# Combining the range flag on VectorE, reading it earlier, and splitting the last PSUM copy between VectorE and ScalarE

## The chip, the cores and the metric

The kernel runs on one core of a Trainium2 chip. TensorE (PE in the profile) multiplies matrices into the accumulator memory PSUM; VectorE (DVE), ScalarE (ACT) and GpSimd (POOL) work element by element on PSUM and on the on-chip memory SBUF; SyncE (SP) issues DMA transfers and computes nothing. Each engine runs its own instruction queue in order, and semaphores tie the queues together. The metric is the device time of one execution in microseconds (us).

## The reference

The reference is attention inside chunks of 64 positions, followed by a two-layer feed-forward block with an exact GELU. There are 8 batches, 8 heads, 576 positions (nine chunks) and 64 channels a head.

```python
scores = scale * np.matmul(q_c, k_c.transpose(0, 1, 2, 4, 3))
scores = scores - np.max(scores, axis=-1, keepdims=True)
attn = np.exp(scores)
attn = attn / (np.sum(attn, axis=-1, keepdims=True) + 1e-09)
out = np.matmul(attn, v_c)
...
x = np.ascontiguousarray(attn_out.transpose(0, 2, 1, 3)).reshape(B * S, H * D)
h = x @ w_in
g = 0.5 * h * (1.0 + erf(h * inv_sqrt2))
return (g @ w_out).astype(np.float32)
```

x is 4608 x 512, w_in 512 x 2048, w_out 2048 x 512, all float32.

## The kernel before

The 4608 rows are worked through in nine tiles of 512 rows: tiles 0 to 7 hold the first eight chunks of one batch each, tile 8 the ninth chunk of all eight batches. For a tile the kernel makes the scores, takes exp without subtracting the maximum, divides by the sums, and sends the result through the two layers in bf16. From tile 1 on, both layers are computed by seven block products instead of eight (a Strassen scheme), so VectorE makes sums and differences of blocks, and results are put together from products. The order on each engine is written out by hand: tables of step names (`LAST` is that of tile 8) and hooks that hang work on the slots of the second layer.

**The last tile's second layer** (`mm2_seven`) has seven steps of two slots each, 14 slots numbered from 0; a slot is eight matmuls of 128 x 256 into one PSUM tile `y_ps`, accumulated. For the last tile the bank called "a" is two PSUM tiles, one for each 128 rows. A step's result is copied by ScalarE into a `kept` buffer (L721), or added by VectorE to such a buffer (L726), which `store_block` then stores (L874). The last step ends in `last_piece`, once for each 128 rows: VectorE copies the 128 x 256 result out of PSUM (L978), and two transfers of 64 KB store it, one issued by SyncE, one by ScalarE (L981).

**The range flag.** Leaving out the maximum is exact enough only while the sums are in range. All reciprocals of sums stay in SBUF in three places. At slot 6 of the last tile's second layer, `range_test` takes their minima and maxima on VectorE (L885), compares these with 2^-40 and 2^40 (L886, L887), and reduces the comparisons to one value a partition, 1 for good (L888). After the last step `range_count` adds the 128 values by a matmul with ones (L894), and VectorE casts the sum to an integer (L895). All five engines then load it into a register (`values_load`, L1337) and branch (L1338): below 128, the whole computation is done once more in a general way (`general`), which these inputs do not need; else they go to the end of the program, where SyncE waits for every semaphore in turn and all engines meet.

Of the kernel before, what the change touches and what calls it, by code (L numbers as in the profile page):

```python
# [11 lines left out]
def kernel(  # L12
# [9 lines left out]
    nc = tc.nc  # L22
    P = 128
    f32 = mybir.dt.float32
    bf16 = mybir.dt.bfloat16
# [7 lines left out]
    G = H // 2  # L33
# [27 lines left out]
    QD = P // G  # L61
# [17 lines left out]
    NB = MT // 32  # L79
    late = rest[:].bitcast(f32)[:, 256 - 14 * NB:256]  # L80
    homes = [None, ident_f[:], late]
# [26 lines left out]
    work = ctx.enter_context(tc.tile_pool(name="work", bufs=3))  # L108
# [5 lines left out]
    ps_at = ctx.enter_context(tc.tile_pool(name="ps_at", bufs=3, space=bass.MemoryType.PSUM))  # L114
# [329 lines left out]
    DV, AC, PO = nc.vector.tensor_copy, nc.scalar.copy, nc.gpsimd.tensor_copy  # L444
# [84 lines left out]
    HD = d_model // 2  # L529
    HM = MT // P // 2  # L530
# [343 lines left out]
            by.dma_start(rows.rearrange("m p d -> p m d"), y_sb[i * CH:(i + 1) * CH])  # L874

    LOW, HIGH = 2.0 ** -40, 2.0 ** 40
    verdict = []

    def range_test():

        assert used == [h.shape[-1] for h in homes]
        n = len(homes)
        for a, op in enumerate((mybir.AluOpType.min, mybir.AluOpType.max)):
            for i, home in enumerate(homes):
                nc.vector.tensor_reduce(ends[:, a, i:i + 1], home, axis=mybir.AxisListType.X, op=op)  # L885
        nc.vector.tensor_scalar(ok[:, 0:n], ends[:, 0], LOW, None, op0=mybir.AluOpType.is_gt)  # L886
        nc.vector.tensor_scalar(ok[:, n:2 * n], ends[:, 1], HIGH, None, op0=mybir.AluOpType.is_lt)  # L887
        nc.vector.tensor_reduce(good, ok, axis=mybir.AxisListType.X, op=mybir.AluOpType.min)  # L888
        verdict.append(good)

    def range_count():

        count = ps_at.tile([1, 1], f32, tag="at", name="count")
        nc.tensor.matmul(count[:], ones_1, verdict[0], start=True, stop=True)  # L894
        nc.vector.tensor_copy(total, count[:])  # L895

    def general():

# [76 lines left out]

    def last_piece(t, m, y_ps):
        y_sb = ypool.tile([P, HD], f32, tag="y", name="y_sb")
        DV(y_sb[:], y_ps)  # L978
        for i in range(P // CH):
            m0 = ((HM + m) * (P // CH) + i) * S + MT  # L980
            (nc.sync if i == 0 else nc.scalar).dma_start(out[m0:m0 + CH, 0:HD], y_sb[i * CH:(i + 1) * CH])  # L981
# [47 lines left out]
    def phase(t, extra2, by_rows=False, first=0, extra1={}, seven=False):  # L1029
        nms = MT // P  # L1030
        order = [(ms, qt) for ms in range(nms) for qt in range(NQ)]
        if by_rows:
            order = [(None, f) for f in range(FF - FC)] + [(ms, NQ - 1) for ms in range(nms)]
        if t not in DENSE:
            mm1_seven(t, extra1)
        else:
            for f in range(first, FF):
                for u in extra1.get(f, ()):
                    u()
                mm1_slot(t, f)  # L1040
        if seven:
            mm2_seven(t, extra2)
            return
        for s, (ms, qt) in enumerate(order):
            for u in extra2.get(s, ()):
                u()
            if ms is None:
                mm2_rows(t, qt)
            else:
                mm2_slot(t, ms, qt)  # L1050
        for u in extra2.get("end", ()):
            u()
# [33 lines left out]
    act_scratch = consts.tile([P, 1], f32, name="act_scratch")  # L1086
    small = consts.tile([P, 28], f32, name="small")
    ends = small[:, 0:6].rearrange("p (a i) -> p a i", a=2)
    ok, good, ones_1 = (small[:, 6:11].bitcast(bf16)[:, a:b] for a, b in ((0, 6), (6, 7), (7, 8)))
    total = small[0:1, 11:12].bitcast(mybir.dt.int32)  # L1090
    nc.gpsimd.memset(ones_1, 1.0)
    homes[0] = consts.tile([P, 3 * NB + 16 + 2 * NB], f32, name="early")[:]

    def act_table(func):
# [2 lines left out]
    with tc.manual_schedule():  # L1097
# [158 lines left out]
        for t in range(1, NT):  # L1256
            n = t + 1
            if n < NT:
                tiles[n]["x"] = xpool.tile([P, G, MT], bf16, tag="x", name="x")
            if t == 2:  # L1260
                sums_home()
            if t in STEPS:
                play(t, STEPS[t])
                continue
            if t == 1:
                mm1_slices(1, {0: mm, 1: at, 2: at, 3: mm, 8: mm},
                           (((0, 1, 2), (0,)), last_av, ((0, 1, 2), (1,)), ((3,), (0, 1)), ((8,), (0, 1)),
                            ((0, 1, 2, 3, 8), (2,)), ((0, 3, 8, 1, 2), (3,))))
                x_sums(1)
                for g in range(G):  # L1270
                    cast_qk(2, "k", g, DV)
                flip(2, "q")
                load_v_rows(2, (0,))
                flip(2, "k")
                for ms, y_sb in held:
                    store(0, ms, y_sb)
                held.clear()
                load_v_rows(2, (1,))
                cast_v_rows(2, PO)
                bring_qk(3)  # L1280
            if t > T0 and n + 1 < NT:
                flip_qk(n + 1)
            def next_loads():
                if t + 3 == NT - 1:
                    bring_qk(t + 3)
                elif t + 3 < NT:
                    bring_qk(t + 3)
                if n + 1 < NT:
                    load_v_rows(n + 1)
                    cast_v_rows(n + 1, PO)  # L1290
            if t == T0:
                flip(n + 1, "q")
            elif t > T0:
                next_loads()
            e1, e2 = {}, {}
            exp, gelu = lambda: act_table(Act.Exp), lambda: act_table(Act.Gelu)
            xs = [lambda m=m: quad_x(n, m // 2, m % 2) for m in range(G)]
            g = [[lambda i=i, a=a: g_sum(t, i, a) for i in (1, 2, 4)] for a in range(2)]
            parts = [[lambda m=m: quad_part(t + 2, m // 2, m % 2) for m in ms] for ms in ((1, 0), (3, 2))]
            e1 = {"s3": [lambda: g_sum(t, 3)], "g0": g[0]} if t not in DENSE else {9: [lambda: g_sum(t, 3)], 13: g[0]}  # L1300
            e2 = {0: g[1][:2], 2: g[1][2:]}
            if t <= T0:
                ov = [lambda m=m: quad_over(n, m) for m in range(G)]
                rx = [[lambda m=m: att_rc(n, m), lambda m=m: quad_x_plain(n, m)] for m in range(G)]
                e2 = {0: [exp, lambda: quad_scores(n, ALONE)] + g[1][:2], 2: g[1][2:],
                      4: [lambda: [quad_sums(n), quad_turned(n)]], 5: [ov[0]], 6: [ov[1]],
                      7: [ov[2]] + rx[0], 8: [ov[3]] + rx[1], 9: rx[2], 10: rx[3]}
                e2[{1: 7, 2: 5, T0: 6}[t]].insert(1, lambda: quad_av(n, ALONE))
                if t > 1:
                    e1["x"] = [lambda: x_sums(t)]  # L1310
                if t == T0:
                    e1["g0"] = g[0][:1] + [lambda: w_in_sums(3, (0, 1))] + g[0][1:] + [lambda: w_in_sums(3, (2, 3))]
                if t == 1:
                    e1["w"] = [lambda: weight_sum(2), lambda: weight_sum(3)]
                    e1["w0"] = [lambda: w_in_sums(0, (0, 1))]
                    e1["w1"] = [lambda: w_in_sums(0, (2, 3))]
                    e2[2].append(lambda: weight_sum(4))
                    e2[4].append(lambda: load_qk(4, "q"))
                    e2[7].append(lambda: pool_cast_qk(4, "q"))
                    e2[12] = [lambda: flip_qk(3), lambda: load_qk(4, "k"), lambda: pool_cast_qk(4, "k"),  # L1320
                              lambda: load_v_rows(3), lambda: cast_v_rows(3, PO)]
                else:
                    e1["k"] = [lambda: flip_qk(n + 1) if t < T0 else flip(n + 1, "k"), next_loads]
                if t < T0:
                    e2[11] = [gelu]
                else:
                    e2[2] += [lambda: g_sum(t, 3)]
                    e2[10] += [lambda: quad_scores(n + 1, BETWEEN), gelu]
                    e2[12] = [lambda: x_sums(n)] + parts[0]
                    e2[13] = parts[1]  # L1330
            if t in WHOLE:
                e1, e2 = whole_hooks(t)
            if t == NT - 1:
                e2.setdefault(6, []).append(range_test)
            phase(t, e2, first=5 if t == 1 else 0, extra1=e1, seven=True)
        range_count()
        in_range = nc.values_load(total)  # L1337
        with tc.If(in_range < P, preferred_fallthrough_block=False):  # L1338
            general()
# [1 line left out]
_INS = ['q', 'k', 'v', 'moe_w_in', 'moe_w_out']  # L1341
# [26 lines left out]
```

## Time and profile before

| | us |
|---|---|
| Median of three runs (lowest, highest) | 266.9 (266.48, 267.42) |
| The profiled execution's own time | 267.09 |
| Its span, first to last instruction | 265.5 |
| TensorE busy in the span | 256.1 |
| VectorE busy | 223.1 |
| ScalarE busy | 190.5 |
| GpSimd busy | 103.2 |

Busy times are of instructions that compute. Loading a register, branching, waiting for a semaphore and issuing a DMA are a sequencer's work and are not counted there; the profile shows them under names such as SPq or ACTq, by line. In a timeline row stand the start, the duration, engine, line, operation, result and source. In a row of groups, the count is followed by total busy time and the mean in ns, then by the idle time before.

### The profile page before, as it was taken

What the parts mean: (1) busy time and instruction counts of PE and PEld (TensorE: products, weight loads), DVE (VectorE), ACT (ScalarE), POOL (GpSimd) and SP (SyncE); (2) the same over time, 40 slices, a digit from 0 to 9 for tenths busy, and PEclk for the clock granted to TensorE, in tenths of its full rate; (3) what the DMA queues carried; (4) which work ended last, traced back from release to release, by engine and by line L of the source; (5) the groups of instructions that cost most, each with busy time, mean ns of one, the idle gap of its engine ahead of it and who ended that gap; (6) DMA issues with size and microseconds to landing.
All of it is one profiled execution on the core that took longest, in us unless ns stands there. A gap on an engine that the chain in (4) does not pass through costs nothing.

```text
span 265.5 us, 7854 instructions
## 1 busy us (share of the span) xinstructions
PE 256.1 (96%) x3122; PEld 210.6 (79%) x3122; DVE 223.1 (84%) x394; ACT 190.5 (72%) x386; POOL 103.2 (39%) x225
## 2 busy tenths in 40 slices
PE   6789999999999999999999999999999999999993
PEld 2478875556888888887888888888888888888882
DVE  6874986898897599678999999999999999948772
ACT  3856758987767987898888588947894789227720
POOL 7767778702364291481372095009411300000000
PEclk9999999999999999999999999999999999999998
DMA  6999998999979979999999988998973410130014
GB/s 201 268 311 396 395 401 236 283 193 289 243 195 284 220 175 244 275 239 249 276 245 232 267 186 237 217 175 195 264 160 80 134 42 2 41 119 3 2 40 125
DMA packets 123416, 54.02 MB, mean 203 GB/s; under 512 B 97776, under 2 KB 120304, under 8 KB 123376
## 3 DMA queue, kind: packets, MB, share of 16 engines
q1 hardware_dynamic: 123072, 53.23, 77.4%
q8 instruction: 25, 0.41, 0.7%
q10 hardware_dynamic: 304, 0.26, 0.3%
q14 instruction: 15, 0.12, 0.1%
HBM read 36.70 MB, written 9.44 MB: 174 GB/s over the span
## 4 chain that ended last, share of the span: by engine, by line
PE 76%; DMA 10%; ACT 7%; SPq 4%; issue 1%; DVE 0%; POOL 0%
PE hs_ps L601 31%; PE y_ps L761 22%; PE y_ps L791 13%; DMA arrival<-in_moe_w_out_dram 8%; ACT h L609 3%; SPq L181 2%; PE h_ps L491 2%; DMA arrival<-in_moe_w_in_dram 2%; PE av_ps L349 2%; PE h_ps L481 2%; ACT pT L272 2%; SPq L142 1%; PE y_ps L1025 1%; PE y_ps L989 1%; PE s_ps L264 1%; ACT L1095 1%
## 5 line engine op out<-in xcount | busy, mean ns | idle before, releaser
L609 ACT ACTIVATE h<-hs_ps 128x512 bf16<-128x512 f32 x87 | 49.6, 609 | 6.5 <-PE hs_ps L601 5.7
L238 POOL CAST v_nat<-arrival 128x256 bf16<-128x256 f32 x56 | 24.9, 473 | 33.5 <-DMA arrival<-in_v_dram 23.1
L601 PEld LDWEIGHTS <-w_in_sb 128*128 128x128 bf16 x348 | 33.9, 98 | 4.7 <-issue 0.2
L194 POOL CAST q_nat<-arrival 128x256 bf16<-128x256 f32 x40 | 16.8, 467 | 50.2 <-DMA arrival<-in_k_dram 25.3
L601 PE MATMUL hs_ps<-x,w_in_sb 128*128 128x256 bf16 x232 | 31.8, 272 | 0.0
L761 PEld LDWEIGHTS <-h 128*128 128x128 bf16 x240 | 23.2, 98 | 2.8
L1095 ACT ACT_TABLE_LOAD x16 | 20.5, 1283 | 1.3 <-PEq L1352 1.0
L190 POOL CAST k_nat<-arrival 128x256 bf16<-128x256 f32 (+1 forms) x44 | 19.1, 476 | 5.3 <-DMA arrival<-in_k_dram 5.3
L721 ACT COPY kept<-y_ps 128x512 f32<-128x512 f32 (+1 forms) x17 | 9.0, 536 | 16.0 <-PE y_ps L761 15.9
L761 PE MATMUL y_ps<-w_out_sb,h 128*128 128x256 bf16 x160 | 18.6, 273 | 0.0
L761 PE MATMUL y_ps<-v_bd,k_bd 128*128 128x256 bf16 x160 | 18.5, 273 | 0.1
L761 PEld LDWEIGHTS <-k_bd 128*128 128x128 bf16 x160 | 15.6, 98 | 2.1 <-issue 0.2
L618 ACT COPY hs_ps<-hs_ps 128x512 f32<-128x512 f32 x29 | 16.2, 583 | 0.6 <-PE hs_ps L601 0.5
L601 PE MATMUL hs_ps<-k_bd,w_in_sb 128*128 128x256 bf16 x116 | 16.6, 272 | 0.0
L493 ACT ACTIVATE h<-h_ps 128x512 bf16<-128x512 f32 x21 | 12.5, 604 | 5.5 <-PE h_ps L465 4.1
L272 ACT ACTIVATE pT<-s_ps 128x512 bf16<-128x512 f32 x28 | 14.4, 599 | 1.8 <-PE s_ps L264 1.8
L791 PEld LDWEIGHTS <-h 128*128 128x128 bf16 x144 | 13.8, 98 | 1.7
L465 PE MATMUL h_ps<-x,w_in_sb 128*128 128x256 bf16 x128 | 14.5, 273 | 0.1
L601 PE MATMUL hs_ps<-k_bd,w_in_more 128*128 128x256 bf16 x96 | 14.2, 273 | 0.0
L601 PEld LDWEIGHTS <-w_in_more 128*128 128x128 bf16 x128 | 12.5, 98 | 2.0 <-issue 0.3
L726 DVE TENSOR_TENSOR kept<-y_ps,kept 128x512 f32<-128x512 f32 (+1 forms) x16 | 10.4, 651 | 4.3 <-PE y_ps L761 2.3
L465 PEld LDWEIGHTS <-w_in_sb 128*128 128x128 bf16 x128 | 12.3, 98 | 2.1 <-DVE w_in_sb L1070 0.7
(175 smaller groups left out, 638.9 us busy)
## 6 DMA issues: line engine op xcount, KB each, us to landing
arrival<-in_v_dram SPq DMA_DIRECT2D x58, 128.0 KB, 3.2
arrival<-in_k_dram SPq DMA_DIRECT2D x28, 256.0 KB, 5.6
arrival<-in_q_dram SPq DMA_DIRECT2D x7, 1024.0 KB, 6.9
out_dram<-kept SPq DMA_DIRECT2D x24, 256.0 KB, 3.2
arrival<-in_moe_w_out_dram SPq DMA_DIRECT2D x4, 1024.0 KB, 12.1
arrival<-in_moe_w_in_dram SPq DMA_DIRECT2D x6, 512.0 KB, 8.5
out_dram<-y_sb SPq DMA_DIRECT2D x8, 256.0 KB, 2.5
arrival<-in_v_dram SPq DMA_DIRECT2D x28, 64.0 KB, 2.7
```

The lines of the kernel that those rows point to most:

```text
L190: copy(st[nm][:, q0:q0 + n, g], st[nm + "f"][:, 2 * q0:2 * (q0 + n), g].rearrange("p (q r) d -> p q r d", r=2))
L194: copy(st[nm][:, g, j:j + 2].rearrange("p j r d -> p r j d"), st[nm + "f"][:, 2 * g:2 * g + 2, j:j + 2])
L238: copy(st["v"][:, r::2, n], st["vf"][:, r::2, n])
L272: nc.scalar.activation(pT[:].rearrange("p u (c j) -> p u c j", j=J), tiles[t]["s_ps"][m // 2][m % 2][:].rearrange("p u (j c) -> p u c j", ...
L465: nc.tensor.matmul(to[:, cols], left, right[:, cols], start=(start and a == 0), stop=stop, skip_group_check=True)
L493: nc.scalar.activation(tiles[t]["h"][:, f, :], h_ps[:], Act.Gelu)
L601: nc.tensor.matmul(hs[:, f], left[:, ks, f * P:(f + 1) * P], right[:, ks], start=(fresh and f == 0 and ks == 0), stop=(ks == 1), skip_grou ...
L609: nc.scalar.activation(h[:, n:n + HM, HD * c:HD * (c + 1)], src, Act.Gelu)
L618: "s11": lambda: AC(place_of("b")[:], bank["a"][:]),
L761: nc.tensor.matmul(to, left(f, m), right[:, f], start=(fresh and (split or m == 0) and f == 0), stop=(f == HF - 1), skip_group_check=True)
L791: nc.tensor.matmul(bank[name][:, m], left(f, m), right[:, f], start=(fresh and m == 0 and f == 0), stop=(f == HF - 1), skip_group_check=True)
L1095: nc.scalar.activation(act_scratch[:], rest[:, 0:1], func)
```

## The change

`range_test` goes further on VectorE: it transposes the 128 values of the flag within blocks of 32 partitions (L889 of the changed kernel), takes the minimum of each row (L890), combines the four blocks' minima one at a time (L892), and writes an integer `bad`, 1 if the flag is below 0.5 (L893). The matmul with ones, its cast and the ones themselves are gone. The register is loaded at three places in the program: by SyncE and GpSimd at the end of `range_test`, by ScalarE at slot 10, by TensorE and VectorE after the last step. The branch takes the general way if the register is not zero. In `last_piece` the last 128 rows are copied in two halves of 128 columns, the first by VectorE, the second by ScalarE.

```diff
     def range_test():
...
-        nc.vector.tensor_reduce(good, ok, axis=mybir.AxisListType.X, op=mybir.AluOpType.min)
-        verdict.append(good)
-
-    def range_count():
-
-        count = ps_at.tile([1, 1], f32, tag="at", name="count")
-        nc.tensor.matmul(count[:], ones_1, verdict[0], start=True, stop=True)
-        nc.vector.tensor_copy(total, count[:])
+        nc.vector.tensor_reduce(good, ok, axis=mybir.AxisListType.X, op=MIN)
+        turned = work.tile([P, NB, 32], f32, tag="rc", name="turned", bufs=4)[:, 0]
+        nc.vector.transpose(turned, good.to_broadcast([P, 32]))
+        nc.vector.tensor_reduce(good, turned, axis=mybir.AxisListType.X, op=MIN)
+        for s in range(1, G):
+            nc.vector.tensor_tensor(good[0:1], good[0:1], good[QD * s:QD * s + 1], op=MIN)
+        nc.vector.tensor_scalar(bad, good[0:1], 0.5, None, op0=mybir.AluOpType.is_lt)
+        read_flag((mybir.EngineType.SP, mybir.EngineType.Pool))
+
+    flag = nc.alloc_registers("flag")
+
+    def read_flag(engines):
+        for reg in flag:
+            if reg.engine in engines:
+                nc.reg_load(reg, bad)
...
     def last_piece(t, m, y_ps):
         y_sb = ypool.tile([P, HD], f32, tag="y", name="y_sb")
-        DV(y_sb[:], y_ps)
+        n = HD // 2 if m == HM - 1 else HD
+        DV(y_sb[:, 0:n], y_ps[:, 0:n])
+        if n < HD:
+            AC(y_sb[:, n:HD], y_ps[:, n:HD])
...
-    nc.gpsimd.memset(ones_1, 1.0)
...
             if t == NT - 1:
                 e2.setdefault(6, []).append(range_test)
+                e2.setdefault(10, []).append(lambda: read_flag((mybir.EngineType.Activation,)))
             phase(t, e2, first=5 if t == 1 else 0, extra1=e1, seven=True)
-        range_count()
-        in_range = nc.values_load(total)
-        with tc.If(in_range < P, preferred_fallthrough_block=False):
+        read_flag((mybir.EngineType.PE, mybir.EngineType.DVE))
+        with tc.If(flag, preferred_fallthrough_block=False):
             general()
```

SyncE's queue at the end of the program, before. `kept` are sums of the last tile that are stored, `y_sb` its last rows, `small` the buffer that holds the flag; what a row waits for stands in brackets, by engine or by DMA queue.

```order
L874 DMA out_dram<-kept 64x2x256 [waits DMAHW0_49]
L874 DMA out_dram<-kept 64x2x256 [waits DMAHW1_49,DVE_49]
L874 DMA out_dram<-kept 64x2x256 [waits DMAHW2_49]
L874 DMA out_dram<-kept 64x2x256 [waits DMAHW4_49,DVE_49]
L981 DMA out_dram<-y_sb 64x256 [waits DMAHW6_49,DVE_49]
L981 DMA out_dram<-y_sb 64x256 [waits DMAHW0_49,DVE_49]
L1337 TENSOR_LOAD small [waits DVE_49]
L1338 COMPARE_AND_BRANCH
```

And after:

```order
L874 DMA out_dram<-kept 64x2x256 [waits DMAHW0_49]
L901 TENSOR_LOAD small [waits DVE_49]
L874 DMA out_dram<-kept 64x2x256 [waits DMAHW1_49,DVE_49]
L874 DMA out_dram<-kept 64x2x256 [waits DMAHW2_49]
L874 DMA out_dram<-kept 64x2x256 [waits DMAHW4_49,DVE_49]
L990 DMA out_dram<-y_sb 64x256 [waits DMAHW6_49,DVE_49]
L990 DMA out_dram<-y_sb 64x256 [waits DMAHW0_49,Activation_49]
L1346 COMPARE_AND_BRANCH
```

The load moved from behind the last store to ahead of the stores of the second `kept` buffer, five stores earlier, and the last store waits for ScalarE (Activation) where it waited for VectorE.

ScalarE's queue at the same place, before:

```order
L874 DMA out_dram<-kept 64x2x256 [waits DVE_49,Activation_49]
L981 DMA out_dram<-y_sb 64x256 [waits DVE_49]
L981 DMA out_dram<-y_sb 64x256 [waits DMAHW7_49,DVE_49]
L1337 TENSOR_LOAD small [waits DVE_49]
L1338 COMPARE_AND_BRANCH
```

And after:

```order
L901 TENSOR_LOAD small [waits DVE_49]
L874 DMA out_dram<-kept 64x2x256 [waits DVE_49,Activation_49]
L990 DMA out_dram<-y_sb 64x256 [waits DVE_49]
L987 COPY y_sb<-y_ps 128x128 [waits DMAHW7_49,DMAHW0_49,DVE_49]
L990 DMA out_dram<-y_sb 64x256 [waits Activation_49]
L1346 COMPARE_AND_BRANCH
```

The load now stands ahead of ScalarE's three stores, and a copy of 128 columns, which waits for VectorE, between the last two.

VectorE's queue from the last reduction of the range test to the next add, after (before, the same reduction was followed by that add at once):

```order
L887 TENSOR_REDUCE small<-small 128x1 [waits DVE_49]
L889 STREAM_TRANSPOSE turned<-small 128x32 [waits DVE_49]
L890 TENSOR_REDUCE small<-turned 128x1 [waits DVE_49]
L892 TENSOR_TENSOR small<-small 1x1 [waits DVE_49] x3
L893 TENSOR_SCALAR small<-small 1x1 [waits DVE_49]
L726 TENSOR_TENSOR kept<-y_ps,kept 128x512 [waits DMAHW5_49,PE_49,Activation_49]
```

Six instructions came in between, each of which waits for VectorE's own semaphore.

More of the change, by code (lines that the diff above doesn't have):

```diff
@@ L876 @@
     LOW, HIGH = 2.0 ** -40, 2.0 ** 40
-    verdict = []
     def range_test():
         assert used == [h.shape[-1] for h in homes]
-        n = len(homes)
+        MIN, n = mybir.AluOpType.min, len(homes)
         for a, op in enumerate((mybir.AluOpType.min, mybir.AluOpType.max)):
@@ L1088 @@
     ends = small[:, 0:6].rearrange("p (a i) -> p a i", a=2)
-    ok, good, ones_1 = (small[:, 6:11].bitcast(bf16)[:, a:b] for a, b in ((0, 6), (6, 7), (7, 8)))
-    total = small[0:1, 11:12].bitcast(mybir.dt.int32)
-    nc.gpsimd.memset(ones_1, 1.0)
+    ok, good = small[:, 6:12], small[:, 12:13]
+    bad = small[0:1, 13:14].bitcast(mybir.dt.int32)
     homes[0] = consts.tile([P, 3 * NB + 16 + 2 * NB], f32, name="early")[:]
```

## The prediction

> **What bounds the kernel now.** I read four views in this order: the page's busy shares and its chain, then the timeline of the last microseconds engine by engine, then the rows of the lines that only the sequencers run (flag load, branch, final waits), then the DMA landings. Changed work lies only at the end, so the first view has to say whether anything before it matters.
>
> ```profile
> span 265.5 us, 7854 instructions
> PE 256.1 (96%) x3122; PEld 210.6 (79%) x3122; DVE 223.1 (84%) x394; ACT 190.5 (72%) x386; POOL 103.2 (39%) x225
> 248.99 12.24 PE y_ps L761 x112
> 261.26 0.42 DVE y_sb L978
> 261.68 0.05 DVE small L895
> ```
>
> TensorE is busy 96% of the span, and the chain is TensorE to 261.2 us. So a change at the end can touch two things: whether TensorE is held up in its last steps, and what follows 261.2. After that the span has another 4.3 us (265.5 less 261.2), in which hardly any engine is busy. The chain view stops at 261.7 because sequencer work isn't in it, so I asked for it by line.
>
> ```profile
> 261.26 0.42 DVE L978 COPY y_sb<-y_ps 128x256 f32<-128x256 f32 x1 [0.45 <-PE y_ps L761]
> 261.60 0.13 DVE L895 CAST small<-count 1x1 int32<-1x1 f32 x1
> 261.71 0.49 SPq L981 DMA_DIRECT2D out_dram<-y_sb  x1
> 261.71 0.55 ACTq L981 DMA_DIRECT2D out_dram<-y_sb  x1
> L1337 POOLq TENSOR_LOAD <-small x1: 587/587/587, 261.8 to 261.8; - x1
> L1337 SPq TENSOR_LOAD <-small x1: 952/952/952, 262.2 to 262.2; - x1
> L1338 SPq COMPARE_BRANCH  x2: 38/50/61, 263.3 to 263.4; - x2
> L1363 SPq EVENT_SEMAPHORE  x12: 28/28/28, 263.9 to 264.6; - x12
> L1363 SPq DRAIN  x1: 13/13/13, 264.7 to 264.7; - x1
> ...
> out_dram<-y_sb SPq DMA_DIRECT2D x1, 64.0 KB, 1.9
> out_dram<-y_sb ACTq DMA_DIRECT2D x1, 64.0 KB, 2.2
> ```
>
> The reader is to see SyncE's own sequence. It issues the last store at 261.71, loads the flag from 262.2 to 263.2, branches at 263.3 and 263.4, reaches the end block at 263.9, and walks twelve waits to 264.6, after which the closing barrier takes the rest. The last two stores, issued at 261.71, land 1.9 and 2.2 us later, at 263.6 and 263.9. So when the walk reaches most of its waits the stores have landed: the sequencer's flag read and branch set the end, not the transfers. The count itself is not late: VectorE has it at 261.73, while SyncE is issuing until 262.2.
>
> **The change part by part.** First, the flag read leaves SyncE's end: in the order shown with the change it stands ahead of five stores, and the last store now waits for ScalarE. Call T the issue of that store. Before, the walk ends at T + 2.9 (264.6 less 261.71). After, SyncE is free for the branch at T + 0.5; from its first compare to the walk it took 0.6 (263.3 to 263.9), so the walk begins at T + 1.1 and meets transfers still under way. What is late next is the landing: T + 1.9 for SyncE's store. The twelve waits are 0.064 us apart (0.7 over 11 gaps). In the built program the fifth of them holds the semaphore of SyncE's last store and the twelfth that of ScalarE's, so seven gaps (0.45) follow the landing: T + 2.35, with ScalarE's at T + 2.2 inside it. That is 0.55 less. Bounds: were the store's wait first in the walk, T + 2.6 (0.3 less); were only the landing of 2.2 to count, 0.7 less.
>
> Second, T itself moves, since the last copy is split. In the order ScalarE's half (L987) waits for VectorE and for no matmul: it stands behind VectorE's half, and so the two halves run one after the other.
>
> ```profile
> L978 DVE COPY y_sb<-y_ps 128x256 f32<-128x256 f32 x2 | 0.8, 424 | 0.9 <-PE y_ps L761 0.9
> L613 DVE COPY kept_p<-hs_ps 128x512 f32<-128x512 f32 x2 | 1.4, 684 | 2.0 <-PE hs_ps L601 2.0
> L721 ACT COPY kept<-y_ps 128x256 f32<-128x256 f32 x4 | 1.4, 377 | 0.8 <-PE y_ps L761 0.8
> L721 ACT COPY kept<-y_ps 128x512 f32<-128x512 f32 x13 | 7.6, 584 | 15.2 <-PE y_ps L761 15.1
> L981 ACTq DMA_DIRECT2D out_dram<-y_sb x2: 553/600/648, 260.8 to 261.7; - x2
> ```
>
> VectorE pays (684 - 424)/256 = 1.02 ns a column, so 128 columns take 0.424 - 0.130 = 0.29 us; ScalarE pays 0.81 ns, so 0.377 - 0.104 = 0.27. With 0.03 from an end to the next start (the copy ends at 261.68, the store is issued at 261.71), T = 261.26 + 0.29 + 0.03 + 0.27 + 0.03 = 261.88, 0.17 later. Bounds: side by side, T = 261.58, 0.13 earlier; each half as dear as its 256-column row, 262.12, 0.41 later. I take 0.17, by the slopes of the same operations. Even without the wait ScalarE would not start at 261.26, since its previous store holds its queue from 260.84 for 0.65 us, to 261.49. The Trainium skill (PSUM — Partial Sum Buffer, section on PSUM bank collisions) says that reads by VectorE and ScalarE from one bank and quadrant collide and have to be kept apart, disjoint columns too. The wait in the order agrees with that; by it the sum takes +0.17, and without it -0.13 with ScalarE idle.
>
> Third, VectorE combines the flag by six small instructions, each waiting for the one before, which the order shows between the last reduction (L888 before) and the add at L726.
>
> ```profile
> 256.33 0.17 DVE L887 TENSOR_SCALAR small<-small 128x3 bf16<-128x3 f32 x1
> 256.54 0.16 DVE L888 TENSOR_REDUCE small<-small 128x1 bf16<-128x6 bf16 x1
> 257.82 1.24 DVE L726 TENSOR_TENSOR kept<-y_ps,kept 128x512 f32<-128x512 f32 x2 [1.12 <-PE y_ps L761]
> L410 DVE STREAM_TRANSPOSE rc<-rb 128x512 f32<-128x512 f32 x15 | 10.6, 705 | 1.4 <-ACT rb L336 1.2 <-ACT rb L403 0.2
> L287 DVE STREAM_TRANSPOSE pt<-pT 128x256 f32<-128x256 f32 x16 | 6.9, 434 | 0.0
> L895 DVE CAST small<-count 1x1 int32<-1x1 f32 x1 | 0.1, 134 | 0.0
> L726 DVE TENSOR_TENSOR kept<-y_ps,kept 128x512 f32<-128x512 f32 x1 | 0.7, 693 | 1.1 <-PE y_ps L761 1.1
> L726 DVE TENSOR_TENSOR kept<-y_ps,kept 128x256 f32<-128x256 f32 x2 | 0.8, 424 | 0.6 <-PE y_ps L761 0.4
> L761 PE MATMUL y_ps<-v_bd,h x16: 272/272/273, 259.3 to 260.9; 128*128 128x256 bf16 x16
> ```
>
> The transpose: 0.434 - 224 x 1.06 ns = 0.20. The reduction of 32 columns: 0.18, a little over the 0.16 of L888. The four single-element steps have no row of their kind; between 0.13 (the cast) and 0.17 (L887), 0.16 each. A dependent step began 0.04 after the one before ended. So 0.20 + 0.18 + 4 x 0.16 + 6 x 0.04 = 1.26 us, from 256.70 to 257.96, in an idle stretch that ended at 257.82: the add starts 0.14 late. Its cover: the first add takes 0.69 us, to 258.51, and the pair ends at 259.06, so the second (0.42) began at 258.64 and the first has 0.13 us to spare; TensorE's last step begins at 259.3 in the bank that the second frees, which is another 0.24. Cost 0. If the cover went, each further microsecond would reach TensorE whole.
>
> Fourth, what the moved loads hold up. SyncE's load starts at about 257.96 and takes between 0.59 (POOL's row) and 0.95 (its own, right behind a store); I take 0.6, as its queue is idle then. Behind it stand the stores of the first add, which went out at 258.54 and 259.19, and of the second pair at 259.96:
>
> ```profile
> 256.01 0.37 ACT L721 COPY kept<-y_ps 128x256 f32<-128x256 f32 x1 [0.50 <-PE y_ps L761]
> 258.54 1.25 SPq L874 DMA_DIRECT2D out_dram<-kept  x2
> 259.96 0.59 SPq L874 DMA_DIRECT2D out_dram<-kept  x1
> 260.02 0.74 ACTq L874 DMA_DIRECT2D out_dram<-kept  x1
> ```
>
> The add itself is done at 258.66 now, so they go 0.14 later, or 0.4 later by the dear load. The next y_sb store, due at 260.83, is met either way (258.91 + 3 x 0.6 + gaps = 260.8). ScalarE's load sits between its last copy (done at 256.4) and 260.02: hidden. POOL has no work left; TensorE's and VectorE's loads follow their last work, as before. Gone with no gain are the count matmul and its cast, since SyncE was issuing until 262.2, and a one-column memset on POOL at the start, which is 0% of the chain.
>
> Sum: -0.55 + 0.17 + 0 = -0.38 us on the profiled execution's 267.09 (its span 265.5 and 1.6 around it). That one is 0.19 above the median of 266.9, so I forecast 266.9 - 0.38 = 266.5 us. 0.3% of this kernel is 0.8 us, about what a measurement can tell from no change; the forecast is within it.
>
> **The rivals.** (a) Side by side: the halves do not queue on each other. For it: both read 128 columns of their own. Against: the wait, and ScalarE's issue to 261.49. It gives -0.55 - 0.13, 266.2.
>
> (b) The gain is eaten by the transfers, and the change so doesn't shorten the end. For it:
>
> ```profile
> 259.60:261.60 2.00, 1.71 (x16) 1.28 (x14) 1.10 (x4) 0.00 (x0) 0.00 (x0) 1.00 0.71 169
> 261.60:263.50 1.90, 0.00 (x0) 0.00 (x0) 0.13 (x2) 0.00 (x0) 0.00 (x0) 1.00 0.80 235
> ...
> DMA to landing us min/median/max: 1.9/2.2/2.4
> ```
>
> The last stores run with the DMA engines 71% and 80% busy; stores that go out up to 0.4 us later share the same end. Against: the four y_sb stores land in 1.9 to 2.4 us, the last pair no later than the pair ahead of it. If the landing slips by 0.38 the time is 266.9.
>
> (c) More than I count: only the landing of 2.2 limits (-0.7), and T holds or comes earlier (0 to -0.13): 266.1 or a little less, the faster side.
>
> (d) Slower: the small steps on VectorE are dearer than their rows. Place: the add at 257.82. It reaches TensorE when the chain passes 1.12 + 0.13 + 0.24 = 1.49 us, 0.25 a step, and makes the kernel slower than before at 1.87 (0.31 a step), by 0.8 us at 2.67 (0.44 a step, a 256-column transpose's price); then 267.7. Against: the 0.13 to 0.17 of the nearest rows.
>
> (e) The branch is slower among the stores. SyncE's jump took 0.5 (263.4 to 263.9) when the transfers were ending; now it falls at about 262.5, among them.
>
> ```profile
> q14 instruction: 3, 0.02, 2.5%
> q8 instruction: 1, 0.02, 2.1%
> ```
>
> In the last 3 us the one packet of the instruction queue q8 took 2.1% of 16 engines, 1.0 us. The walk's fifth wait would be reached at T + 1.35 and the landing is at T + 1.9, so a jump may take 0.55 more unseen: one such packet is free, two in a row (2.0) start the walk at T + 2.6 and end it at T + 3.3, 0.95 above the forecast: 267.5. Beside it the Trainium skill (Runtime: NRT & Kernel Launch, section on instruction fetch mechanics): a taken branch outside the fetched window stalls for a DMA of the target page.
>
> **How the numbers follow.** Forecast 0.50, (a) 0.10, (b) 0.15, (c) 0.12, (d) 0.07, (e) 0.06. Faster by over 0.3%: (c), and as much again from (a) and the forecast, whose bounds reach 266.1: 0.22. Slower: most of (d) and (e) with the dear ends of the split, 0.10. Same: 0.68. The range takes in (a), (b) and most of (c): with the 0.9 us that three runs of one kernel already spread (266.48 to 267.42), 265.9 to 267.2; outside remain parts of (c), (d) and (e).
>
> **What would show it.** In the changed kernel's profile: SyncE's flag load near 258.0 with about 0.6 us; ScalarE's L987 starting after VectorE's L985 ends, near 261.6, and the last stores issued near 261.9; SyncE's end waits starting near 263.0 and finishing near 264.2; the six small VectorE rows ending by 258.0 and TensorE's last y_ps step still starting at 259.3. I am wrong if the last step starts later, if the walk still begins after 263.8, or if the last landing takes clearly over 2.2 us.

## The result

The changed kernel takes 268.15 us in the median of 16 runs (267.15 to 269.12), the kernel before 266.81 (265.98 to 267.81). The ratio is 1.0042, with a 95% interval of 1.0026 to 1.0058: slower by 0.7 to 1.5 us, where 0.4 us less was forecast. Nearly everything in the forecast's sum came out; one term that it held fixed, the time a store takes to land, did not.

The profiled execution of the changed kernel (268.19 us, its span 266.6) shows this in its last microseconds. First the timeline, columns as before:

```profile
258.00 0.14 DVE L893 TENSOR_SCALAR small<-small 1x1 int32<-1x1 f32 x1
258.11 1.21 DVE L726 TENSOR_TENSOR kept<-y_ps,kept 128x512 f32<-128x512 f32 x2
...
261.51 0.29 DVE L985 COPY y_sb<-y_ps 128x128 f32<-128x128 f32 x1 [0.45 <-PE y_ps L761]
261.88 0.27 ACT L987 COPY y_sb<-y_ps 128x128 f32<-128x128 f32 x1 [5.24 <-DVE y_sb L985]
262.17 0.50 ACTq L990 DMA_DIRECT2D out_dram<-y_sb  x1
```

Then the rows of the flag loads, of the branches, and of SyncE's walk through the twelve end waits (here the whole walk, behind it the same line asked for up to 264.5 us and up to 265.3 us only, and last the row that has TensorE's first instruction behind its branch, a DRAIN at 262.0):

```profile
L901 SPq TENSOR_LOAD <-small x1: 469/469/469, 258.2 to 258.2; - x1
L901 PEldq TENSOR_LOAD <-small x1: 513/513/513, 260.3 to 260.3; - x1
L1346 PEldq COMPARE_BRANCH  x2: 90/200/310, 260.9 to 261.7; - x2
L1346 SPq COMPARE_BRANCH  x2: 38/50/61, 262.7 to 262.8; - x2
L1371 SPq EVENT_SEMAPHORE  x12: 28/28/28, 263.3 to 265.7; - x12
...
L1371 SPq EVENT_SEMAPHORE  x4: 28/28/28, 263.3 to 263.5; - x4
...
L1371 SPq EVENT_SEMAPHORE  x5: 28/28/28, 263.3 to 265.3; - x5
...
L1371 PEldq DRAIN  x2: 8/160/311, 262.0 to 266.2; - x2
```

SyncE reaches its walk 1.1 us after the last store's issue, as forecast (263.3 less 262.17). But it gets through only four waits; the fifth, for its own last store, opens at 265.3, and the twelfth comes at 265.7, 3.5 us after the issue. The kernel before took 2.9. The landings say why:

```profile
DMA to landing us min/median/max: 2.3/3.1/3.2
...
out_dram<-y_sb SPq DMA_DIRECT2D x1, 64.0 KB, 3.1
out_dram<-y_sb ACTq DMA_DIRECT2D x1, 64.0 KB, 3.2
```

Before, these two stores landed 1.9 and 2.2 us after issue. What kept them stands in the DMA queues. Packets, MB and share of the 16 DMA engines, first from 263.0 to 264.25 us, then from 264.1 to 265.0:

```profile
q1 hardware_dynamic: 77, 0.06, 19.8%
q10 hardware_dynamic: 85, 0.07, 19.7%
q8 instruction: 1, 0.02, 6.1%
q14 instruction: 2, 0.02, 3.9%
...
q1 hardware_dynamic: 5, 0.00, 3.6%
q10 hardware_dynamic: 5, 0.00, 1.8%
```

One instruction packet on queue q8 took 6.1% of 16 engines in 1.25 us: 1.22 us, nearly a whole engine for the whole window. It starts at 263.01 and so ends at 264.23. From 264.04 to 264.21 no store packet starts; then come five packets of each store queue (q1 is SyncE's, q10 ScalarE's). A store of 64 KB is 64 rows of 1 KB, four to each of 16 engines, and a flag write each: five packets are one engine's share. The trace doesn't name a packet's engine, but the count and the moment fit one reading: fifteen engines had delivered their part in time, and the one with the instruction packet delivered last. (The two packets of q14 start at 264.04 and 264.07, when the other shares are through; an experiment below has the same hold without them.) In the kernel before, the packet came later, and so did TensorE's branch, which is in the last row:

```profile
q14 instruction: 3, 0.02, 7.0%
q8 instruction: 1, 0.02, 5.8%
...
L1338 PEldq COMPARE_BRANCH  x2: 91/198/304, 262.5 to 262.8; - x2
```

The queue rows are of the kernel before from 263.8 to 264.9: 1.0 us of q8 again (5.8% of 16 times 1.1), with no store packet left in the window. Little was to spare: the last store packet starts before 263.6, q8's at 263.84.

The packet follows a branch, and TensorE's is the branch that fits. In the kernel before TensorE branched from 262.5 to 262.8, since its flag came from VectorE's cast at 261.7. Now it loads the flag at 260.3, while its matmuls still run, and branches from 260.9 to 261.7 (rows above). The sequence on one engine moved ahead by 1.1 us and q8's packet by 0.8, onto the last stores. The profile shows no wait of TensorE for this packet: its first instruction behind the branch runs at 262.0, a microsecond before the packet starts.

### The profile page after: what moved, and what is told of

It is laid out like the page before. It is cut to its first block, busy times and chain, and to the rows that moved or that the text cites. A ratio compares the mean times of both kernels' runs of the same rounds, so it can differ in the third digit from the quotient of the medians.

```text
span 266.6 us, 7851 instructions
## 1 busy us (share of the span) xinstructions
PE 255.9 (96%) x3115; PEld 210.9 (79%) x3121; DVE 224.5 (84%) x399; ACT 190.8 (72%) x387; POOL 102.8 (39%) x224
## 4 chain that ended last, share of the span: by engine, by line
PE 75%; DMA 12%; ACT 7%; SPq 2%; issue 1%; DVE 0%; ACTq 0%; POOL 0%
PE hs_ps L601 31%; PE y_ps L761 22%; PE y_ps L791 13%; DMA arrival<-in_moe_w_out_dram 8%; ACT h L609 3%; PE h_ps L491 2%; DMA arrival<-in_moe_w_in_dram 2%; SPq L181 2%; DMA arrival<-in_q_dram 2%; PE av_ps L349 2%; PE h_ps L481 2%; ACT pT L272 2%; PE y_ps L1034 1%; PE y_ps L998 1%; PE s_ps L264 1%; ACT L1103 1%
## 5 line engine op out<-in xcount | busy, mean ns | idle before, releaser
L605 DVE TENSOR_TENSOR hs_ps<-hs_ps,kept_p 128x512 f32<-128x512 f32 x15 | 10.3, 691 | 3.5 <-PE hs_ps L601 3.1
```

## The experiments

Three theories of the late landing: **fetch**, that q8's packet behind TensorE's branch holds them, as above; **crowding**, that the stores behind SyncE's early flag load go out later and crowd the last ones; **two writers**, that a buffer written by two engines is slow to store. Each run below was compared with the kernel before on the same chip.

**The flag part alone.** `last_piece` of the kernel before, the rest as changed:

```diff
-        n = HD // 2 if m == HM - 1 else HD
-        DV(y_sb[:, 0:n], y_ps[:, 0:n])
-        if n < HD:
-            AC(y_sb[:, n:HD], y_ps[:, n:HD])
+        DV(y_sb[:], y_ps)
```

> The flag part of the change alone: the last 128 rows are copied by VectorE whole, as before. Three theories of why the last stores land 3.1 us after their issue. Fetch: TensorE branches earlier, and the 16 KB packet that then fetches its program stands ahead of the last stores on one DMA engine. Crowding: the stores behind SyncE's early flag load go out later and crowd the last ones. Two writers: a buffer written by two engines is stored more slowly. Fetch expects the slow landing to stay: the packet goes as in the changed kernel, about 1.5 us after TensorE's last matmul, the last store is issued 0.17 to 0.2 us earlier, and the landing is still at about the same moment (3 us or a little more after issue); time within 0.3 us of the changed kernel's, about 0.3 to 0.4% above before. Crowding expects the same to 0.2 us. Two writers expects landings of 1.9 to 2.2 us and a time 0.5 us below before.

Measured: 1.0058 (1.0032 to 1.0084), stores landing late with one engine writing them. The rows of the stores, the walk, and q8 from 262.0 to 263.4:

```profile
DMA to landing us min/median/max: 2.3/2.8/3.3
...
L1368 SPq EVENT_SEMAPHORE  x12: 27/28/28, 262.2 to 264.7; - x12
...
q8 instruction: 1, 0.02, 5.3%
```

Two writers falls, and the loss is in the flag part. Fetch and crowding expected the same here.

**The split alone.** The kernel before with the four lines of the split.

> The kernel before with the last copy split between VectorE and ScalarE, the flag as before. By my prediction's working the two halves follow each other and the last store is issued 0.17 us later, with the flag load and the branch behind it: 0.17 us above before, a ratio of 1.0006. Fetch and crowding expect landings of 1.9 to 2.4 us as before; two writers expects about 3 us, 0.5 us or more above before.

Measured: 0.9998 (0.9975 to 1.0020). The halves do run one after the other, and landings are as before:

```profile
260.55 0.29 DVE L979 COPY y_sb<-y_ps 128x128 f32<-128x128 f32 x1 [0.45 <-PE y_ps L761]
260.91 0.27 ACT L981 COPY y_sb<-y_ps 128x128 f32<-128x128 f32 x1 [5.23 <-DVE small L895]
261.20 0.50 ACTq L984 DMA_DIRECT2D out_dram<-y_sb  x1
...
DMA to landing us min/median/max: 2.0/2.2/2.3
```

From the start of VectorE's copy to the store's issue it is 0.65 us (261.20 less 260.55), against 0.45 before: 0.20 us later. The ratio allows that (0.20 us is 1.0007) and can't show it.

**TensorE reads late, in a buffer of its own.** VectorE writes the flag again four times after its last copy, and TensorE and VectorE load that:

```diff
+    late_flag = consts.tile([P, 2], f32, name="late_flag")
+    bad_late = late_flag[0:1, 0:1].bitcast(mybir.dt.int32)
...
+    def flag_again(times):
+        for _ in range(times):
+            nc.vector.tensor_scalar(bad_late, good[0:1], 0.5, None, op0=mybir.AluOpType.is_lt)
...
-        read_flag((mybir.EngineType.PE, mybir.EngineType.DVE))
+        flag_again(4)
+        read_flag((mybir.EngineType.PE, mybir.EngineType.DVE), bad_late)
```

> The changed kernel, but VectorE writes the flag again four times after its last copy, and TensorE (and VectorE) load that late flag; SyncE, ScalarE and GpSimd read early as in the change. Fetch expects TensorE's 16 KB packet to start about 0.8 us or more later than in the changed kernel, after the last stores' packets; the last stores land 1.9 to 2.3 us after issue; the end then comes as the prediction had it: 0.2 to 0.4 us below before, about 1.1 to 1.4 us below the changed kernel. Crowding and two writers expect no difference to the changed kernel: landings of 3 us, about 0.4% above before.

and its control, where TensorE loads the early flag:

```diff
-        read_flag((mybir.EngineType.PE, mybir.EngineType.DVE))
+        read_flag((mybir.EngineType.PE,))
+        flag_again(4)
+        read_flag((mybir.EngineType.DVE,), bad_late)
```

> The control to the run above: the same four extra writes on VectorE after its last copy, and VectorE loads the late flag, but TensorE loads the early one as in the change. All three theories expect the changed kernel's time (about 0.4% above before) and landings of 3 us. If this kernel is fast too, it was VectorE's branch or the extra writes, not TensorE's, that mattered.

Measured: 1.0191 (1.0161 to 1.0221) and 1.0236 (1.0212 to 1.0261). Between the two, 1.2 us go the way of fetch, but both are slow for a reason that no theory had, and the expected times were missed by about 5 us. In both, the last tile already begins late: its `y_ps` steps start at 251.99 us in the first and at 253.12 in the second, in the changed kernel at 249.25, before any changed instruction.

```profile
251.99 12.24 PE y_ps L761 x112
```

The new buffer moved all buffers that are allocated behind it by 32 bytes a partition, the landing buffers of the loads among them. So both were made again with `bad_late` in a spare column of the flag's own buffer:

```diff
+    bad_late = small[0:1, 14:15].bitcast(mybir.dt.int32)
```

**TensorE reads late, no buffer moved.**

> The changed kernel with TensorE's and VectorE's flag written again four times after VectorE's last copy, as in the run before it, but held in a spare column of the buffer that holds the flag, so that no other buffer moves. Fetch: TensorE's 16 KB packet starts after the last stores' packets, these land 1.9 to 2.3 us after issue, the walk isn't held, and the time is 0.2 to 0.5 us below before, a ratio of about 0.9985. Crowding and two writers: landings of 3 us, ratio 1.004 as the changed kernel. If the slow front of the run before was not the moved buffers but the extra instructions, this one is 3 to 5 us slower than before as well.

Measured: 0.9979 (0.9953 to 1.0005), 266.58 us. The branches, the landings, the walk, and the instruction queues from 262.4 to 264.7 and from 264.7 to 266.0:

```profile
L1352 PEldq COMPARE_BRANCH  x2: 90/200/310, 263.4 to 263.7; - x2
...
DMA to landing us min/median/max: 2.0/2.3/2.5
...
L1377 SPq EVENT_SEMAPHORE  x12: 27/28/28, 263.7 to 264.9; - x12
...
q14 instruction: 1, 0.01, 1.1%
...
q8 instruction: 1, 0.02, 6.0%
```

The last store goes out at 262.5 here. TensorE branches 1.2 us after it in place of 0.5 ahead of it, q8's packet comes behind the stores, they land in 2.0 and 2.3 us, and the walk ends 2.4 us after the issue, what the prediction worked out (2.35). SyncE's early load is as in the changed kernel, and so are its four stores ahead of the last, issued 3.3 to 1.1 us before it in both, so crowding falls.

**Its control, TensorE early.**

> The control: the same four extra writes and VectorE's late load, with TensorE's early load as in the change, the buffers in their old places. All theories: landings of 3 us or more, ratio about 1.004. Fetch: the difference between this one and the run above it is the cost of TensorE's early read, 1.1 to 1.5 us.

Measured: 1.0040 (1.0015 to 1.0065), 268.37 us, the changed kernel's time. With the last store at 261.6:

```profile
L1353 PEldq COMPARE_BRANCH  x2: 90/200/310, 260.3 to 261.1; - x2
...
DMA to landing us min/median/max: 2.3/2.8/3.4
...
L1378 SPq EVENT_SEMAPHORE  x12: 27/28/28, 262.8 to 265.4; - x12
```

The two differ in which copy of the flag TensorE loads, and by 1.8 us in the medians (0.6% in the ratios; fetch expected 1.1 to 1.5 us). It is TensorE's early read with its branch, and neither VectorE's branch nor the extra writes.

**TensorE's early read alone.** SyncE, ScalarE, GpSimd and VectorE load a late copy, as in the kernel before; the last copy isn't split:

```diff
-        read_flag((mybir.EngineType.SP, mybir.EngineType.Pool))
...
+        read_flag((mybir.EngineType.PE,))
+        flag_again(2)
+        read_flag((mybir.EngineType.DVE, mybir.EngineType.SP, mybir.EngineType.Pool, mybir.EngineType.Activation), bad_late)
```

> TensorE's early read alone: the flag is combined on VectorE and TensorE loads it as in the change, while SyncE, ScalarE, GpSimd and VectorE load a copy that VectorE writes after its last copy; the last copy isn't split. SyncE's end is then as in the kernel before (load, branch, walk), which reached the fifth wait 2.5 us after the last store's issue. Fetch: the store lands about 3.2 us after its issue, so the walk stands at the fifth wait for 0.5 to 0.7 us: ratio 1.002 to 1.003. Crowding: SyncE's stores go out as before, landings of 1.9 to 2.4 us, ratio 1.000.

Measured: 1.0046 (1.0021 to 1.0072). The last store goes out at 261.04. The landings, the walk, q8 from 261.9 to 263.3, and the branches of TensorE and VectorE:

```profile
DMA to landing us min/median/max: 2.3/3.2/3.3
...
L1373 SPq EVENT_SEMAPHORE  x12: 27/28/28, 263.2 to 264.7; - x12
...
q8 instruction: 1, 0.02, 5.4%
...
L1348 PEldq COMPARE_BRANCH  x2: 90/200/310, 259.9 to 260.7; - x2
L1348 DVEq COMPARE_BRANCH  x2: 51/53/55, 261.9 to 262.1; - x2
```

The walk ends 3.6 us after the issue, against 2.9: 0.7 us of the 1.2 that the ratio gives. One engine's earlier branch is enough to slow the kernel. The rest of the difference lies inside the interval (0.6 to 1.9 us) and wasn't followed.

This run also shows whose packet q8's is. It starts at 262.08, and by then only TensorE has both its branch instructions behind it; the second one of the others starts at 262.1 (VectorE), 262.4, 262.7 and 262.8. The packets of q14 don't hold the stores: the first of them starts at 263.25, when q8's packet (to 263.29) has held one engine for all but its end, and the ten late store packets start from 263.28 on. In all four profiles with TensorE's early read (the changed kernel, the flag part alone, the control above and this one) the first of the last ten store packets begins within 0.02 us of the end of q8's packet.

**What was to be the best version**, without the split: the late copy written once, or four times.

> What the above would make the best version: flag combined on VectorE, SyncE, ScalarE and GpSimd reading early, TensorE and VectorE reading a copy of it that VectorE writes once after its last copy, and the last copy not split. Fetch: the packet starts about where it did before, after the stores have been read out; no stall; by the prediction's working without the split 0.55 us below before, ratio 0.998, and about 0.6% below the changed kernel. Crowding: landings of 3 us, ratio 1.003 or more.

> The flag combined on VectorE, SyncE, ScalarE and GpSimd reading early, TensorE and VectorE reading a copy written four times after VectorE's last copy; the last copy not split. Fetch: TensorE's packet starts about 2.8 us after the last store's issue, clear of it; walk's twelfth wait at 2.4 us after issue; 0.5 us below before, ratio 0.998. It differs from the late-flag run with the split copy by the 0.17 us of the split. Were TensorE's later branch to hold the end, the ratio would be 1.000 or more.

Measured: 0.9988 (0.9965 to 1.0011) and 0.9983 (0.9957 to 1.0009). In the first the landings are 2.0 to 2.4 us and the walk ends 2.4 us after the store's issue at 260.7:

```profile
L1374 SPq EVENT_SEMAPHORE  x12: 28/28/28, 261.9 to 263.1; - x12
```

So the 0.5 us are there in the profile (2.4 against 2.9). In time, all three versions with the late read lie below the kernel before (0.9979, 0.9988, 0.9983), and each interval still holds 1: they beat the changed kernel, and were not told from the kernel before one by one. Which of the three is best can't be said.

**The moved buffers.** The changed kernel with an unused buffer ahead of the flag's, of 32 and of 64 bytes a partition:

```diff
+    spare = consts.tile([P, 8], f32, name="spare")
     small = consts.tile([P, 28], f32, name="small")
```

> The changed kernel with an unused buffer of 32 bytes a partition ahead of the flag's buffer, so that every buffer from there on stands 32 bytes higher and the loads' landing places are no longer multiples of 64 bytes. The late-flag run with its own new buffer had all of this, and lost 3 to 5 us long before the last tile. If the place of the buffers did that: 1.5 to 2.5% above before, loads of v landing in about 4.2 us in place of 3.3. If it was the extra instructions: 1.004, as the changed kernel.

> The same with 64 bytes, so that the buffers move twice as far but stay at multiples of 64 bytes. If the multiple of 64 matters: 1.004, as the changed kernel. If any move of the buffers matters: 1.5% above before or more.

Measured: 1.0193 (1.0150 to 1.0235) and 1.0223 (1.0184 to 1.0261), so keeping to multiples of 64 bytes does not help; both places cost 4 to 5 us more than the changed kernel's. It is the place of the buffers and not the extra instructions. SyncE's transfers, the loads from HBM among them, keep the DMA engines longer for the same packets and bytes. First the changed kernel, then the one with 64 bytes:

```profile
q1 hardware_dynamic: 123072, 53.23, 76.4%
arrival<-in_v_dram SPq DMA_DIRECT2D x58, 128.0 KB, 3.3
arrival<-in_k_dram SPq DMA_DIRECT2D x8, 128.0 KB, 3.8
```

```profile
q1 hardware_dynamic: 123072, 53.23, 87.1%
arrival<-in_v_dram SPq DMA_DIRECT2D x58, 128.0 KB, 3.8
arrival<-in_k_dram SPq DMA_DIRECT2D x8, 128.0 KB, 7.5
```

In the kernel before, the landing buffers begin at multiples of 256 bytes in each partition, and a row of v or k is 256 bytes; moved by 32 or 64, each row crosses such a boundary. The Trainium skill (DMA: Bandwidth & Descriptors, section on how a descriptor splits into AXI transactions) says that a transaction can read less than 256 bytes but must start at a multiple of 256, so that a transfer which doesn't start there begins at the multiple below. It says this of reading; what moved here is the place that is written. The two runs would fit the same rule for writing, but they don't show it: no run moves the buffers by 256 bytes, which would tell this cause from another effect of the place.

## Why the prediction was wrong

**The step that failed** is in the first part of the change: "What is late next is the landing: T + 1.9 for SyncE's store." The landing was taken from the kernel before as a constant. It measured T + 3.1, since the change moved TensorE's branch and so the packet behind it. The walk ended at T + 3.5, where T + 2.35 was forecast and T + 2.9 stood before: 0.6 us lost in place of 0.55 gained. The prediction had named this as a sign of being wrong, a last landing clearly over 2.2 us. The control pair shows that the cause is TensorE's early read; that its packet does it rests on the packets' times in the four profiles with that read.

**What had been in view.** The quoted rows held the packet (2.1% of 16 engines in 3 us, 1.0 us), and rival (e) spoke of it. But (e) took it for a packet that SyncE's jump might wait for. It is TensorE's, and SyncE's jump took 0.5 us as before (262.8 to 263.3), with no instruction packet under way but q8's. The question not asked was what the packet does to others: it takes one DMA engine of sixteen for 1.0 to 1.4 us, and a store is done when its slowest engine is. The sentence "TensorE's and VectorE's loads follow their last work, as before" was wrong for TensorE: they had waited for the count, which came after its last matmul, and now the flag is there from 258.14, so the load ran under the matmuls at 260.3. The count matmul and its cast, which I put under "Gone with no gain", were what had held that branch back. In rival (b), that the transfers eat the gain, the landing would slip by 0.38 through crowding; the slip was three times that, and the mechanism another.

**SyncE's flag read**: right. Its load took 0.47 us (forecast 0.6), and it reached the walk at T + 1.1. With the fetch out of the way the walk ends at T + 2.4.

**The split**: right. Serial halves of 0.29 and 0.27 us, as worked out; T came 0.66 us after the start of VectorE's copy, 0.21 later than before (forecast 0.17). The trace agrees with the wait in the order; no run has the two halves side by side, so what a collision would do isn't shown.

**VectorE's six steps**: right. They end at 258.14, forecast 257.96 plus the 0.25 by which this whole execution ran late since before the last tile; the add began at 258.11 (257.82 before), and TensorE's last step was not held: it follows the step ahead at about the same distance (257.8 to 259.6; 257.6 to 259.3 before).

The tail so accounts for 0.6 us later in the walk and 0.2 in T, 0.8 of the 1.1 us between the two profiled spans; the 0.3 us left lie ahead of all changed work and are within what executions of one kernel differ by.

## What to carry to other kernels

A branch can cost twice: the engine that takes it needs time (SyncE 0.5 us here), and the instruction packet that follows takes a DMA engine from whatever transfer is under way. Here TensorE's packet started 1.0 to 1.6 us behind its second branch instruction. When a wait ahead of a branch is removed, find out where the packet will land, and hold the branches of engines with nothing left to do, so that their packets come behind the last stores. Of the engines here only SyncE's branch was on the path, and only TensorE's earlier branch did harm. And a landing time read from a trace holds for the traffic of that trace: look at the instruction queues, not only at the data queues, before you keep it.

## What was not expected of the hardware

One 16 KB instruction packet held a 64 KB store back from a landing at 1.9 us to one at 3.1 us, although by the packet counts fifteen of sixteen DMA engines were done. It came when TensorE had already run its first instruction behind the branch. And an unused buffer of 32 or 64 bytes a partition, which moved the landing buffers off multiples of 256 bytes, cost 4 to 5 us of 268; with 64 bytes the eight 128 KB loads of k landed in 7.5 us in place of 3.8. An experiment that needs one more buffer should take it from spare room, so that nothing else moves.
